# A branch hint, constants as last terms of sums, and a router with fewer vector operations in a fused attention and mixture-of-experts kernel

## The chip, the cores and the metric

One core of one Trainium2 chip. The core has TensorE (PE; its weight loads are shown apart, as PEld), VectorE (DVE), ScalarE (ACT), GpSimd (POOL) and SyncE (SP), which issues most DMAs. Each runs its own list of instructions in order, and semaphores order the lists against each other. The metric is the time of one launch in microseconds (us).

## The reference

Three stages with 4 x 8 heads, 576 tokens a head, 64 wide, so 2304 tokens of 512. Attention has a causal mask and a bias from a running sum of `s`; a softmax row is divided by its sum plus 1e-9. The router takes the largest of 8 logits (`x @ w_gate` plus a bias by the token's modality), and that expert's probability scales the token. Last comes a gated layer.

```python
scores = np.where(causal, -1e9, scores + np.minimum(bias, 0.0))
attn = np.exp(scores - scores.max(-1)); attn /= attn.sum(-1) + 1e-9
logits = x @ w_gate + modality_bias[modality_id]
e_idx = np.argmax(logits, axis=1); probs = softmax(logits)      # its sum + 1e-9
out[e_idx == e] = gate_w * (np.maximum(x @ w1[e], 0) @ w2[e])
out = (sigmoid(x @ w_gate2) * (x @ w_val)) @ w_out
```

## The kernel before, in words

Every product of fp32 numbers is made of three products of a rounded high part and a low remainder, so each operand is split on ACT (high) and on DVE or POOL (low).

**Attention** goes by pairs of heads, 16 of them. The order of its steps is written out by hand: START for the first pairs, then the list PERIOD, gone through once for each pair, with entries shifted by up to four rounds, so that several pairs are under way. `R1` (line 415) adds 1e-9 to the softmax sums of a pair (`rs`), `R2` takes the reciprocal, `N` and `Ns` scale the pair's part of x and of the gate logits (`lg`). `txs` is a matrix product on PE that a router's rank product may ride on. POOL makes the bias tiles (`L174`, `L167`) and the splits of k and v (`L198`, `L202`).

**The router** (`Router.batch`, line 608) runs once for each of 4 batches, after the batch's last `Ns`. It doesn't issue its operations at once: it puts them into a queue, and a `tick` after most DVE steps of PERIOD takes one entry off it. After each operation `gap` empty entries are put in front (1 in batches 0 and 1, 0 in 2 and 3); `space(n)` puts in n more. The operations are: sum of `lg` over head pairs, the modality's bias `tb` added, maximum, one-hot row `oh` of the chosen expert, then `ranks`: with triangular and all-ones matrices PE counts the tokens ahead of each one of its expert. In batches 0 to 2 this product waits for the next `txs` (`side`, `beside`) and holds the queue until then; in batch 3 it is issued where `ranks` stands. Behind it come the copy of the counts, the row number `ix` of each token, the sum of the probabilities and its reciprocal, five indirect table writes on POOL (`tab`, line 675), and two stores of x. In batch 1 a guess of the fullest expert follows (lines 689 to 707), from which the first expert's weights are loaded ahead (`on_guess`). `moe.first` (in period 17) gathers the first rows and splits the first weights on POOL.

**The experts** (`Moe`) take slots of 256 tokens. `early` runs the first two slots, both with the guessed expert; after each of its steps u it calls `main(u)`, which takes all empty entries out of the queue and pumps PUMPS = (9, 0, 0, 14) entries: 9 at u = 0, none at 1 and 2, 14 from 3 on. When the queue is empty, `slots` puts 59 operations in (all at line 774 in the profile), which compute the remaining slots; they must be through by u = 10. `Moe.run` counts its later steps to `last` = 72 and calls `step(u)` behind each; `put(k, ...)` lays a task at step last + k. The last steps, 0 to 8, hold two half slots. `extras` (line 1082) is a block that runs only if there are more tokens for an expert than the main slots hold; otherwise every engine branches over it. Here it isn't run.

**The gated layer** (`Moe2`) follows: Strassen products of 384 tokens (line 1374), the sigmoid on ACT, and the output product (lines 1529, 1580). `preload` loads ACT's table for the sigmoid by an activation of a single column.

Of the kernel before, what the change touches and what calls it, by code (L numbers as in the profile page):

```python
# [54 lines left out]
class Attention:  # L55
# [22 lines left out]
    def setup(self):  # L78
# [23 lines left out]
        for i in range(3):  # L102
            t = self.cp.tile([128, 2, 5], F32, name=f"sums{i}")
            nc.gpsimd.memset(t, 1.0)
            self.sums_t.append(t)
# [193 lines left out]
    def exp(self, n, i):  # L299
        nc, h = self.nc, self.head(n)  # L300
        rows = TS[i]
        nc.scalar.activation(  # L302
            h["P"][i][:rows, : T0[i] + rows], h["P"][i][:rows, : T0[i] + rows], AF.Exp, bias=h["nm", i][:rows], scale=-1.0,
            accum_out=self.sums_t[(n // 2) % 3][:rows, n % 2, POS[i] : POS[i] + 1],
        )
# [107 lines left out]
    def R1(self, p):  # L413
        self.nr[p] = [self.wk.tile([128, 2, 5], F32, tag=t, name=t) for t in ("rs", "ri")]
        self.nc.vector.tensor_scalar(self.nr[p][0], self.sums_t[p % 3], 1e-9, None, ALU.add)

# [79 lines left out]
BF16 = mybir.dt.bfloat16  # L496
SPE = mybir.EngineType.SP
BIG = 100000.0
TROWS, PUMPS = 96, (9, 0, 0, 14)
# [5 lines left out]
class Router:  # L505
    def __init__(self, tc, cp, ap, ps, ident, mod_bias, mod_id, x, tab, B, S):
# [6 lines left out]
        self.oh = [T([128, 6, 8], f"oh{i}", BF16) for i in range(2)]  # L513
        self.lg = [ap.tile([128, 5, 8, 8], F32, name=f"lg{i}") for i in range(2)]
        self.xr = [ap.tile([128, 5, RW], F32, name=f"xr{i}") for i in range(2)]
# [27 lines left out]
        nc.gpsimd.dma_start(self.tab, self.fill[:TROWS])  # L543
        self.cnt = [T([128, 8], f"cnt{i}") for i in range(2)]
        nc.gpsimd.memset(self.cnt[0], 0.0)
        self.k9 = T([128, 9], "k9")
        nc.gpsimd.iota(self.k9, pattern=[[256, 9]], base=128, channel_multiplier=0, allow_small_or_imprecise_dtypes=True)
        self.pidh, self.w256 = T([128, 1], "pidh"), T([128, 1], "w256")
        nc.gpsimd.tensor_copy(self.pidh, self.pid)
        nc.gpsimd.tensor_scalar(self.pidh[HROW : 2 * HROW], self.pid[HROW : 2 * HROW], -float(HROW), None, ALU.add)  # L550
        nc.gpsimd.memset(self.w256, 256.0)
# [53 lines left out]
    def new_x(self, b):  # L605
        return self.xr[b % 2], self.lg[b % 2]

    def batch(self, b, xr, lg):

        nc, cp, T = self.nc, self.cp, self.T  # L610
        V = nc.vector
        oh = self.oh[b % 2]
        cnt, cnt2 = self.cnt[b % 2], self.cnt[(b + 1) % 2]
        tile_ = lambda shape, nm, dt=F32: cp.tile(shape, dt, tag="r_" + nm, name="r_" + nm)
# [6 lines left out]
        L, mx, eq, em = (tile_([128, 5, 8], "L"), tile_([128, 5], "mx"), tile_([128, 5, 8], "eq"), tile_([128, 5], "em"))  # L621
        ex, se = tile_([128, 5, 8], "ex"), tile_([128, 5], "se")
        R, rk = tile_([128, 6, 8], "R"), tile_([128, 5], "rk")
        ix = tile_([128, 5], f"ix{b % 2}", U32)
        c, c1 = tile_([128, 8], "gc"), tile_([128, 8], "gc1")
        iob = self.iota.unsqueeze(1).to_broadcast([128, 5, 8])
        q = self.q
        q.append(lambda: V.tensor_reduce(L.unsqueeze(3), lg, axis=AX.X, op=ALU.add))
        q.append(lambda: V.tensor_tensor(L, L, tb, ALU.add))
        q.append(lambda: V.tensor_reduce(mx.unsqueeze(2), L, axis=AX.X, op=ALU.max))  # L630
# [5 lines left out]
        def mm(rp):  # L636
            if rp is None:
                V.tensor_tensor(R, st["rp"].rearrange("p (t e) -> p t e", e=8), cnt.unsqueeze(1).to_broadcast([128, 6, 8]), ALU.add)
                self.hold = False
                return  # L640
            nc.tensor.matmul(rp, self.tri, oh.rearrange("p t e -> p (t e)"), start=True, stop=False)
            for t in range(5):
                nc.tensor.matmul(
                    rp[:, 8 * t + 8 :].rearrange("p (t e) -> p t e", e=8), self.ones,
                    oh[:, t].unsqueeze(1).to_broadcast([128, 5 - t, 8]), start=False, stop=t == 4,
                )
            st["rp"] = rp
# [11 lines left out]
        self.space(3)  # L659
        q.append(lambda: nc.scalar.activation(ex, L, AF.Exp))  # L660
        self.space(3)
        q.append(lambda: V.tensor_copy(cnt2, R[:, 5]))
        q.append(lambda: V.tensor_tensor(R[:, 0:5], R[:, 0:5], oh[:, 0:5], ALU.mult))
        q.append(lambda: V.tensor_reduce(rk.unsqueeze(2), R[:, 0:5], axis=AX.X, op=ALU.add))
        q.append(lambda: V.scalar_tensor_tensor(out=rk, in0=em, scalar=float(CAP), in1=rk, op0=ALU.mult, op1=ALU.add))
        q.append(lambda: V.tensor_scalar(ix, rk, 8.0 * CAP, None, ALU.add))
        q.append(lambda: V.tensor_reduce(se.unsqueeze(2), ex, axis=AX.X, op=ALU.add))  # L667
        q.append(lambda: V.tensor_scalar(se, se, 1e-9, None, ALU.add))
        q.append(lambda: V.reciprocal(xr[:, :, 512], se))
# [14 lines left out]
        if b == EARLYB - 1:  # L684
# [4 lines left out]
            q.append(lambda: V.tensor_reduce(m, cnt2, axis=AX.X, op=ALU.max))  # L689
            q.append(lambda: V.tensor_tensor(c, cnt2, m.to_broadcast([128, 8]), ALU.is_equal))  # L690
            q.append(lambda: V.scalar_tensor_tensor(out=c, in0=c, scalar=-8.0, in1=self.iota, op0=ALU.mult, op1=ALU.add))
            q.append(lambda: V.tensor_reduce(gf, c, axis=AX.X, op=ALU.min))
            q.append(lambda: V.tensor_scalar(gf, gf, 8.0, None, ALU.add))
            q.append(lambda: V.scalar_tensor_tensor(
                out=self.grow, in0=gf, scalar=float(CAP // 256), in1=self.pid, op0=ALU.mult, op1=ALU.add))
            q.append(lambda: V.tensor_scalar(c1, cnt2, 256.0 * EARLY, None, ALU.max))
            q.append(lambda: V.tensor_tensor(c1, c1, cnt2, ALU.subtract))
            q.append(lambda: V.tensor_tensor(c, self.iota, gf.to_broadcast([128, 8]), ALU.is_equal))
            q.append(lambda: V.tensor_tensor(c, c, c1, ALU.mult))
            q.append(lambda: V.tensor_tensor(cnt2, cnt2, c, ALU.add))  # L700
# [5 lines left out]
            q.append(lambda: self.indices("idx0", self.tid, 16, 576 * EARLYB - 1))  # L706
            q.append(lambda: V.tensor_copy(self.guess_i, gf[0:1]))

# [46 lines left out]
    def slots(self):  # L755
# [6 lines left out]
        V = nc.vector  # L762
        n = self.cnt[self.B % 2]
        gf, pid = self.guess_f, self.pidh
# [10 lines left out]
        op(V.tensor_tensor, cmp, n.unsqueeze(2).to_broadcast([128, 8, 9]), self.k9.unsqueeze(1).to_broadcast([128, 8, 9]), ALU.is_gt)  # L775
        op(V.tensor_scalar, g1, gf, 1.0, None, ALU.add)
        op(V.tensor_reduce, W[:, 0, 1:9].unsqueeze(2), cmp, axis=AX.X, op=ALU.add)
# [112 lines left out]
class Moe:  # L890
# [189 lines left out]
    def extras(self, more, again):  # L1080

        with self.tc.If(more > 0):  # L1082
            tt = self.r.tt
# [672 lines left out]
def kernel(ctx, tc, q, k, v, s, modality_id, moe_w_gate, modality_bias, w1, w2, wg, wv, wo, out):  # L1756
# [10 lines left out]
    with tc.manual_schedule():  # L1767
# [100 lines left out]
        def later():  # L1868
            x, cuts = glu.x_tasks(1, raws1), (0, 3, 7, 9, 12, 15, 18, 18)
            w = [[], [], s0[0], s0[1] + s0[2], s0[3] + s0[4], s0[5], s0[6]]  # L1870
            for k in range(7):
                put(2 + k, w[k] + x[cuts[k] : cuts[k + 1]])
            put(8, [glu.preload])

        put(-5, [first_tokens])
        put(1, [later])
# [53 lines left out]
```

## Time and profile before

| what | us |
|---|---|
| median of 3 runs (lowest, highest) | 940.32 (939.64, 943.79) |
| profiled execution, its own time | 939.85 |
| its span, first to last instruction | 938.1 |
| PE busy | 900.2 |
| DVE busy | 697.7 |
| ACT busy | 548.3 |
| POOL busy | 392.4 |

Busy is a sum over instructions and says nothing of who waits for whom; ends of matmuls are modelled. Attention takes up to about 262 us, the experts to about 515, the gated layer the rest. In timelines a line is the start, the duration, engine, code line and operation, and in brackets the idle time just before it and what ended that. PEclk, or "granted", is TensorE's clock as a share of 2.4 GHz; 0.50 is the lower level, 1.2 GHz.

### The profile page before, as it was taken

How to read it: one execution, taken by the hardware profiler on the slowest of the kernel's cores; microseconds unless marked ns; L12 is line 12 of the kernel's file. 1: busy time of each engine (PE TensorE's matmuls, PEld its weight loads, DVE VectorE, ACT ScalarE, POOL GpSimd, SP SyncE). 2: the span in 40 equal slices, each digit the busy share in tenths (PEclk: the TensorE clock that was granted, in tenths of full speed). 3: DMA queues.
4: the chain of work that ended last, by engine and by line, in shares of the span. 5: the costliest groups of instructions: out<-in, count | busy, mean ns of one | idle time of the engine just before them, and what ended most of it. 6: DMA issues, size and time to landing. Idle time of an engine off the chain costs nothing. (4 is left out here: it accounts for less than half of the span.)

```text
span 938.1 us, 18673 instructions
## 1 busy us (share of the span) xinstructions
PE 900.2 (96%) x6261; PEld 861.7 (92%) x6261; DVE 697.7 (74%) x1569; ACT 548.3 (58%) x1282; POOL 392.4 (42%) x614
## 2 busy tenths in 40 slices
PE   7999999999999999999998899999999999999996
PEld 7899889888899999999987899999999998889996
DVE  5999999999875688867566666767575747868770
ACT  5999899898733656566544555454535345454440
POOL 7988789798642677776610000010001000111111
PEclk9999999999999999999999999999999999999999
DMA  7667559674435558622655322324242308473501
GB/s 174 157 154 168 138 86 130 165 125 121 164 63 88 165 154 263 204 79 81 205 193 201 98 88 87 116 98 129 64 141 79 116 13 299 143 246 98 168 35 45
DMA packets 163871, 125.34 MB, mean 134 GB/s; under 512 B 86737, under 2 KB 147692, under 8 KB 163254
## 3 DMA queue, kind: packets, MB, share of 16 engines
q1 hardware_dynamic: 158566, 112.44, 43.1%
q0 software_dynamic: 3984, 11.32, 4.2%
q8 instruction: 51, 0.84, 0.4%
q14 instruction: 54, 0.44, 0.2%
q10 hardware_dynamic: 1216, 0.30, 0.1%
HBM read 115.95 MB, written 33.23 MB: 159 GB/s over the span
## 5 line engine op out<-in xcount | busy, mean ns | idle before, releaser
L1374 PE MATMUL X<-a,set 128*128 128x384 f32 x864 | 165.7, 340 | 4.1 <-ACTq L1082 3.0
L1374 PEld LDWEIGHTS X<-a,set 128*128 128x128 f32 x864 | 153.1, 189 | 5.9 <-ACTq L1082 3.2
L869 POOL TENSOR_SCALAR dn<-dr 128x256 int8<-128x256 int8 (+1 forms) x60 | 34.1, 569 | 253.7 <-DVE sg L1404 86.4
L932 POOL TENSOR_TENSOR w<-raw,w 128x512 fp32r<-128x512 f32 x56 | 78.9, 1416 | 47.1 <-ACT w L929 44.5
L174 POOL TENSOR_SCALAR bias<-cumB,cumT 128x576 f32<-128x576 f32 (+4 forms) x155 | 82.8, 536 | 24.6 <-DVE nm L293 20.1
L1511 POOL DMA_INDIRECT out_dram<-oy,row x18 | 20.0, 1109 | 169.3 <-ACT oy L1535 92.0
L996 PE MATMUL ph<-xT,w 128*128 128x256 f32 x672 | 89.9, 283 | 0.0
L996 PEld LDWEIGHTS ph<-xT,w 128*128 128x128 f32 x672 | 83.6, 188 | 0.0
L1374 PE MATMUL Y<-a,set 128*128 128x384 f32 x432 | 82.0, 338 | 0.0
L302 ACT ACTIVATE P<-P,nm 128x576 f32<-128x576 f32 (+3 forms) x128 | 79.5, 627 | 2.1 <-DVE nm L293 2.0
L337 DVE TENSOR_TENSOR PL<-pt,PH 128x512 fp32r<-128x512 f32 (+1 forms) x128 | 77.1, 629 | 2.6 <-ACT PH L330 2.2
L1374 PEld LDWEIGHTS Y<-a,set 128*128 128x128 f32 x432 | 76.5, 188 | 0.1
L1383 ACT COPY u<-X 128x384 f32<-128x384 f32 x72 | 34.5, 480 | 61.5 <-PE X L1374 61.4
L293 DVE CUSTOM_DVE_ANT_0 P<-sb,bias 128x320 f32<-128x320 f32 (+3 forms) x128 | 67.2, 548 | 3.2 <-PE sb L284 2.4
L330 ACT CAST PH<-pt 128x512 fp32r<-128x512 f32 (+1 forms) x128 | 64.6, 551 | 7.6 <-PE pt L321 6.2
L321 PE MATMUL pt<-ident,P 128*128 128x128 f32 x448 | 64.6, 278 | 3.6 <-DVE r_se L667 2.0
L932 DVE TENSOR_TENSOR w<-raw,w 128x512 fp32r<-128x512 f32 x56 | 55.0, 982 | 12.2 <-ACT w L929 11.3
L929 ACT CAST w<-raw 128x512 fp32r<-128x512 f32 x112 | 63.6, 620 | 0.0
L1000 ACT ACTIVATE hH<-ph 128x256 fp32r<-128x256 f32 x72 | 27.7, 385 | 61.2 <-PE ph L996 60.1
L284 PE MATMUL sb<-KT,QH 128*128 128x288 f32 (+3 forms) x192 | 56.3, 317 | 6.8 <-DVE nm L293 4.5
L321 PEld LDWEIGHTS pt<-ident,P 128*128 128x128 f32 x448 | 51.0, 141 | 9.7 <-ACT P L302 3.2
L360 PE MATMUL ot<-PH,vhl 128*128 128x512 f32 (+3 forms) x160 | 55.8, 359 | 1.1 <-DVE QL L258 1.0
(318 smaller groups left out, 2385.0 us busy)
## 6 DMA issues: line engine op xcount, KB each, us to landing
raw<-in_moe_w_dram SPq DMA_DIRECT2D x80, 512.0 KB
h<-sg SPq DMA_DIRECT2D x72, 192.0 KB
cumB<-cum_d SPq DMA_DIRECT2D x32, 288.0 KB
hp<-h SPq DMA_DIRECT2D x24, 384.0 KB
qraw<-in_q_dram SPq DMA_DIRECT2D x58, 128.0 KB
dr<-in_moe_w_out_dram SPq DMA_DIRECT2D x12, 511.6 KB
dr<-in_moe_w_gate_dram SPq DMA_DIRECT2D x24, 255.2 KB
dr<-in_moe_w_val_dram SPq DMA_DIRECT2D x24, 255.2 KB
```

The source lines that it names most:

```text
L174: (nc.vector if n in FILLB else nc.gpsimd).tensor_scalar(res[i][:rows], cumB[:rows, :m], -1.0, self.cumT[:rows, i, n : n + 1], ALU.mult, A ...
L284: nc.tensor.matmul(self.sb[:rows, o : o + c1 - c0], X[:, T0[i] : T0[i] + rows], h["KT"][:, c0:c1], start=j == 0, stop=j == 1)
L293: nc.vector.tensor_tensor_reduce(out=pt[:rows, :m], in0=self.sb[:rows, o : o + m], in1=self.bias_t[n][i][:rows], op0=ALU.add, op1=ALU.min, ...
L302: nc.scalar.activation(h["P"][i][:rows, : T0[i] + rows], h["P"][i][:rows, : T0[i] + rows], AF.Exp, bias=h["nm", i][:rows], scale=-1.0, acc ...
L321: nc.tensor.transpose(pt[:, c : c + 128], h["P"][i][:, T0[j] : T0[j] + 128], self.ident)
L330: self.nc.scalar.copy(t[:, :z], pt[:, :z])
L337: self.nc.vector.tensor_tensor(t[:, :z], pt[:, :z], h["H"][u][:, :z].bitcast(F32), ALU.subtract)
L360: nc.tensor.matmul(out[:, q0 : q0 + z - a], w, X[:, a:z], start=k == 0, stop=k == len(mm) - 1, skip_group_check=True)
L929: nc.scalar.copy(v, src)
L932: (eng or nc.vector).tensor_tensor(v, src, h.bitcast(F32), ALU.subtract)
L996: nc.tensor.matmul(ph, w[:, 128 * dc : 128 * dc + 128], x[:, dc], start=k == 0, stop=k == 11)
L1374: self.nc.tensor.matmul(bank, w[:, c], a[:, h, c], start=first and k == 0, stop=k == 5, skip_group_check=True)
```

## The change

- The softmax sums get a second column that holds 1e-9; `R1` is a reduction over the two in place of an addition.
- `lg` gets a ninth term, into which POOL copies the batch's modality bias; the addition behind the reduction goes. A ninth column of `R` holds 8 CAP, and of `ex` 1e-9, so that two more additions go.
- The counts stay in row 5 of `R`, two tiles of which alternate; the copy goes.
- The guess takes nine operations in place of thirteen, in `scalar_tensor_tensor` form; `gf` is now 8 smaller, and users add it back.
- `tc.If(more > 0)` gets a label, and at step 5 SP, PE, DVE and ACT each get an instruction that says that the branch is likely taken. Where the block is skipped, as here, it is.
- `preload` moves from step 8 to step -40.

```diff
@@ -100,8 +100,9 @@
...
         for i in range(3):
-            t = self.cp.tile([128, 2, 5], F32, name=f"sums{i}")
-            nc.gpsimd.memset(t, 1.0)
+            t = self.cp.tile([128, 2, 5, 2], F32, name=f"sums{i}")
+            nc.gpsimd.memset(t[:, :, :, 0], 1.0)
+            nc.gpsimd.memset(t[:, :, :, 1], 1e-9)
             self.sums_t.append(t)
...
@@ -301,7 +302,7 @@
...
             h["P"][i][:rows, : T0[i] + rows], h["P"][i][:rows, : T0[i] + rows], AF.Exp, bias=h["nm", i][:rows], scale=-1.0,
-            accum_out=self.sums_t[(n // 2) % 3][:rows, n % 2, POS[i] : POS[i] + 1],
+            accum_out=self.sums_t[(n // 2) % 3][:rows, n % 2, POS[i], 0:1],
         )
...
@@ -412,7 +413,7 @@
...
         self.nr[p] = [self.wk.tile([128, 2, 5], F32, tag=t, name=t) for t in ("rs", "ri")]
-        self.nc.vector.tensor_scalar(self.nr[p][0], self.sums_t[p % 3], 1e-9, None, ALU.add)
+        self.nc.vector.tensor_reduce(self.nr[p][0].unsqueeze(3), self.sums_t[p % 3], axis=AX.X, op=ALU.add)
...
@@ -495,6 +496,7 @@
...
 SPE = mybir.EngineType.SP
+AHEAD = [SPE] + [getattr(mybir.EngineType, e) for e in ("PE", "DVE", "Activation")]
 BIG = 100000.0
...
@@ -511,7 +513,7 @@
...
         self.oh = [T([128, 6, 8], f"oh{i}", BF16) for i in range(2)]
-        self.lg = [ap.tile([128, 5, 8, 8], F32, name=f"lg{i}") for i in range(2)]
+        self.lg = [ap.tile([128, 5, 8, 9], F32, name=f"lg{i}") for i in range(2)]
         self.xr = [ap.tile([128, 5, RW], F32, name=f"xr{i}") for i in range(2)]
...
@@ -541,12 +543,21 @@
...
         nc.gpsimd.dma_start(self.tab, self.fill[:TROWS])
-        self.cnt = [T([128, 8], f"cnt{i}") for i in range(2)]
-        nc.gpsimd.memset(self.cnt[0], 0.0)
+        self.zero = ap.tile([128, 8], F32, name="zero")
+        nc.gpsimd.memset(self.zero, 0.0)
+        self.R = [p.tile([128, 6, 9], F32, name=f"R{i}") for i, p in enumerate((ap, cp))]
+        for t in self.R:
+            nc.gpsimd.memset(t[:, :, 8], 8.0 * CAP)
+        self.ex = ap.tile([128, 5, 9], F32, name="ex")
+        nc.gpsimd.memset(self.ex[:, :, 8], 1e-9)
         self.k9 = T([128, 9], "k9")
...
         nc.gpsimd.tensor_copy(self.pidh, self.pid)
+        self.pidg = ap.tile([128, 1], F32, name="pidg")
+        nc.gpsimd.tensor_scalar(self.pidg, self.pid, 8.0 * (CAP // 256), None, ALU.add)
+        self.iotam = ap.tile([128, 8], F32, name="iotam")
+        nc.gpsimd.iota(self.iotam, pattern=[[1, 8]], base=-8, channel_multiplier=0, allow_small_or_imprecise_dtypes=True)
         nc.gpsimd.tensor_scalar(self.pidh[HROW : 2 * HROW], self.pid[HROW : 2 * HROW], -float(HROW), None, ALU.add)
...
@@ -605,12 +616,16 @@
...
+    def counts(self, b):
+        return self.R[b % 2][:, 5, 0:8] if b >= 0 else self.zero
+
     def batch(self, b, xr, lg):
...
         oh = self.oh[b % 2]
-        cnt, cnt2 = self.cnt[b % 2], self.cnt[(b + 1) % 2]
+        R = self.R[b % 2]
+        cnt, cnt2 = self.counts(b - 1), self.counts(b)
         tile_ = lambda shape, nm, dt=F32: cp.tile(shape, dt, tag="r_" + nm, name="r_" + nm)
...
@@ -619,14 +634,14 @@
...
         L, mx, eq, em = (tile_([128, 5, 8], "L"), tile_([128, 5], "mx"), tile_([128, 5, 8], "eq"), tile_([128, 5], "em"))
-        ex, se = tile_([128, 5, 8], "ex"), tile_([128, 5], "se")
-        R, rk = tile_([128, 6, 8], "R"), tile_([128, 5], "rk")
+        ex, se, rk = self.ex, tile_([128, 5], "se"), tile_([128, 5], "rk")
         ix = tile_([128, 5], f"ix{b % 2}", U32)
...
         q = self.q
+        q.append(lambda: nc.gpsimd.tensor_copy(lg[:, :, :, 8], tb))
+        self.space(4)
         q.append(lambda: V.tensor_reduce(L.unsqueeze(3), lg, axis=AX.X, op=ALU.add))
-        q.append(lambda: V.tensor_tensor(L, L, tb, ALU.add))
         q.append(lambda: V.tensor_reduce(mx.unsqueeze(2), L, axis=AX.X, op=ALU.max))
...
@@ -635,7 +650,7 @@
...
             if rp is None:
-                V.tensor_tensor(R, st["rp"].rearrange("p (t e) -> p t e", e=8), cnt.unsqueeze(1).to_broadcast([128, 6, 8]), ALU.add)
+                V.tensor_tensor(R[:, :, 0:8], st["rp"].rearrange("p (t e) -> p t e", e=8), cnt.unsqueeze(1).to_broadcast([128, 6, 8]), ALU.add)
                 self.hold = False
...
@@ -657,15 +672,12 @@
...
         self.space(3)
-        q.append(lambda: nc.scalar.activation(ex, L, AF.Exp))
+        q.append(lambda: nc.scalar.activation(ex[:, :, 0:8], L, AF.Exp))
         self.space(3)
-        q.append(lambda: V.tensor_copy(cnt2, R[:, 5]))
-        q.append(lambda: V.tensor_tensor(R[:, 0:5], R[:, 0:5], oh[:, 0:5], ALU.mult))
+        q.append(lambda: V.tensor_tensor(R[:, 0:5, 0:8], R[:, 0:5, 0:8], oh[:, 0:5], ALU.mult))
         q.append(lambda: V.tensor_reduce(rk.unsqueeze(2), R[:, 0:5], axis=AX.X, op=ALU.add))
-        q.append(lambda: V.scalar_tensor_tensor(out=rk, in0=em, scalar=float(CAP), in1=rk, op0=ALU.mult, op1=ALU.add))
-        q.append(lambda: V.tensor_scalar(ix, rk, 8.0 * CAP, None, ALU.add))
+        q.append(lambda: V.scalar_tensor_tensor(out=ix, in0=em, scalar=float(CAP), in1=rk, op0=ALU.mult, op1=ALU.add))
         q.append(lambda: V.tensor_reduce(se.unsqueeze(2), ex, axis=AX.X, op=ALU.add))
-        q.append(lambda: V.tensor_scalar(se, se, 1e-9, None, ALU.add))
         q.append(lambda: V.reciprocal(xr[:, :, 512], se))
...
@@ -687,16 +699,12 @@
...
             q.append(lambda: V.tensor_reduce(m, cnt2, axis=AX.X, op=ALU.max))
-            q.append(lambda: V.tensor_tensor(c, cnt2, m.to_broadcast([128, 8]), ALU.is_equal))
-            q.append(lambda: V.scalar_tensor_tensor(out=c, in0=c, scalar=-8.0, in1=self.iota, op0=ALU.mult, op1=ALU.add))
+            q.append(lambda: V.scalar_tensor_tensor(out=c, in0=cnt2, scalar=m, in1=self.iotam, op0=ALU.is_equal, op1=ALU.mult))
             q.append(lambda: V.tensor_reduce(gf, c, axis=AX.X, op=ALU.min))
-            q.append(lambda: V.tensor_scalar(gf, gf, 8.0, None, ALU.add))
             q.append(lambda: V.scalar_tensor_tensor(
-                out=self.grow, in0=gf, scalar=float(CAP // 256), in1=self.pid, op0=ALU.mult, op1=ALU.add))
-            q.append(lambda: V.tensor_scalar(c1, cnt2, 256.0 * EARLY, None, ALU.max))
-            q.append(lambda: V.tensor_tensor(c1, c1, cnt2, ALU.subtract))
-            q.append(lambda: V.tensor_tensor(c, self.iota, gf.to_broadcast([128, 8]), ALU.is_equal))
-            q.append(lambda: V.tensor_tensor(c, c, c1, ALU.mult))
+                out=self.grow, in0=gf, scalar=float(CAP // 256), in1=self.pidg, op0=ALU.mult, op1=ALU.add))
+            q.append(lambda: V.scalar_tensor_tensor(out=c1, in0=cnt2, scalar=256.0 * EARLY, in1=cnt2, op0=ALU.max, op1=ALU.subtract))
+            q.append(lambda: V.scalar_tensor_tensor(out=c, in0=self.iotam, scalar=gf, in1=c1, op0=ALU.is_equal, op1=ALU.mult))
             q.append(lambda: V.tensor_tensor(cnt2, cnt2, c, ALU.add))
...
@@ -704,7 +712,7 @@
...
             q.append(lambda: self.indices("idx0", self.tid, 16, 576 * EARLYB - 1))
-            q.append(lambda: V.tensor_copy(self.guess_i, gf[0:1]))
+            q.append(lambda: V.tensor_scalar(self.guess_i, gf[0:1], 8.0, None, ALU.add))
...
@@ -760,7 +768,7 @@
...
         V = nc.vector
-        n = self.cnt[self.B % 2]
+        n = self.counts(self.B - 1)
         gf, pid = self.guess_f, self.pidh
...
@@ -773,7 +781,7 @@
...
         op(V.tensor_tensor, cmp, n.unsqueeze(2).to_broadcast([128, 8, 9]), self.k9.unsqueeze(1).to_broadcast([128, 8, 9]), ALU.is_gt)
-        op(V.tensor_scalar, g1, gf, 1.0, None, ALU.add)
+        op(V.tensor_scalar, g1, gf, 9.0, None, ALU.add)
         op(V.tensor_reduce, W[:, 0, 1:9].unsqueeze(2), cmp, axis=AX.X, op=ALU.add)
...
@@ -1079,7 +1087,7 @@
...
-        with self.tc.If(more > 0):
+        with self.tc.If(more > 0, label="more"):
             tt = self.r.tt
...
@@ -1870,8 +1878,9 @@
...
                 put(2 + k, w[k] + x[cuts[k] : cuts[k + 1]])
-            put(8, [glu.preload])
-
+
+        put(-40, [glu.preload])
+        put(5, [lambda: tc.mark_branch_hint_location("more", "LikelyTaken", engines=AHEAD)])
         put(-5, [first_tokens])
...
```

## Rows read from the trace of the kernel before

**Rows 1.** Windows: us, busy us (instructions) of PE, PEld, DVE, ACT, POOL; clock, DMA

```profile
30.00:243.00 213.00, 203.79 (x1516) 186.54 (x1515) 207.36 (x643) 192.32 (x547) 182.98 (x353) 1.00 0.67 146
```

**Rows 2.** Timeline of DVE: the operation `rs` of three of sixteen pairs

```profile
78.47 0.17 DVE L415 TENSOR_SCALAR rs<-sums 128x10 f32<-128x10 f32 x1
...
91.89 0.98 DVE L415 TENSOR_SCALAR rs<-sums 128x10 f32<-128x10 f32 x1
...
108.04 0.17 DVE L415 TENSOR_SCALAR rs<-sums 128x10 f32<-128x10 f32 x1
```

**Rows 3.** Timelines of POOL and of DVE near 98 us

```profile
98.13 1.58 POOL L202 TENSOR_TENSOR vhl<-vraw,vhl 128x640 fp32r<-128x640 f32 x1
...
98.73 1.03 DVE L629 TENSOR_TENSOR r_L<-r_L,tb 128x40 f32<-128x40 f32 x1
```

**Rows 4.** By code line: count, duration in ns (min/median/max), first and last start

```profile
L629 DVE TENSOR_TENSOR r_L<-r_L,tb x4: 190/264/1032, 98.7 to 270.4; 128x40 f32<-128x40 f32 x4
...
L662 DVE COPY cnt<-r_R x4: 151/168/1186, 116.4 to 272.4; 128x8 f32<-128x8 f32 x4
...
L664 DVE TENSOR_REDUCE r_rk<-r_R x4: 175/188/198, 118.8 to 272.7; 128x5 f32<-128x40 f32 x4
...
L666 DVE TENSOR_SCALAR r_ix<-r_rk x4: 172/688/1211, 121.2 to 273.2; 128x5 uint32<-128x5 f32 x4
...
L668 DVE TENSOR_SCALAR r_se<-r_se x4: 164/166/172, 123.7 to 274.8; 128x5 f32<-128x5 f32 x4
...
L697 DVE TENSOR_TENSOR r_gc<-r_gc,cnt x1: 785/785/785, 208.2 to 208.2; 128x8 f32<-128x8 f32 x1
```

**Rows 5.** Timeline of PE and DVE where attention ends and the experts begin

```profile
260.30 1.04 PE L980 MATMUL mtr<-ident,xg 128*128 128x128 f32 x8
...
262.30 1.58 PE L996 MATMUL ph<-xT,ew 128*128 128x256 f32 x11 [0.34 <-DVE xT L986]
...
262.76 0.48 DVE L628 TENSOR_REDUCE r_L<-lg 128x40 f32<-128x320 f32 x1
...
270.44 0.19 DVE L629 TENSOR_TENSOR r_L<-r_L,tb 128x40 f32<-128x40 f32 x1
...
271.84 0.18 PE L641 MATMUL rp<-oh,tri 128*128 128x48 bf16 x1 [0.77 <-DVE oh L634]
```

**Rows 6.** Timeline of ACT and PE at the branch

```profile
515.00 0.59 ACT L1029 COPY yt<-yh 128x512 f32<-128x512 f32 x1 [3.47 <-PE yh L1114]
515.60 1.28 ACT L1278 ACT_TABLE_LOAD   x1
...
517.92 2.19 PE L1374 MATMUL X<-a,set 128*128 128x384 f32 x6 [2.96 <-ACTq L1082]
```

**Rows 7.** Windows: the stretch just behind the branch, columns as in rows 1

```profile
518.00:521.50 3.50, 3.50 (x12) 3.50 (x12) 0.00 (x0) 1.00 (x2) 0.00 (x0) 0.51 0.01 5
```

**Rows 8.** Groups of instructions by line: count | busy us, mean ns | idle before

```profile
L415 DVE TENSOR_SCALAR rs<-sums 128x10 f32<-128x10 f32 x16 | 6.6, 411 | 0.5
```

**Rows 9.** Timeline of POOL: its first instruction behind the setup

```profile
8.50 0.73 POOL L198 TENSOR_SCALAR vhl<-vraw 128x640 fp32r<-128x640 f32 x1 [1.17 <-DVE cumT L129]
```

**Rows 10.** By code line: the branch over the spare slots (q: an engine's sequencer)

```profile
L1082 SPq EVENT_SEMAPHORE  x9: 17/17/17, 519.6 to 520.2; - x9
...
L1082 ACTq EVENT_SEMAPHORE  x2: 17/17/17, 517.9 to 517.9; - x2
...
L1082 PEldq COMPARE_BRANCH  x1: 3357/3357/3357, 513.0 to 513.0; - x1
```

**Rows 11.** Timeline of SP and ACT behind the branch

```profile
520.48 2.11 SPq L1295 DMA_DIRECT2D xs<-x  x4
...
528.04 0.84 ACT L1309 CAST a<-xs 128x768 fp32r<-128x768 f32 x1
```

**Rows 12.** The page's groups: busy us, mean ns | idle before, and what ended it

```profile
L1000 ACT ACTIVATE hH<-ph 128x256 fp32r<-128x256 f32 x72 | 27.7, 385 | 61.2 <-PE ph L996 60.1
```

## The prediction

> **What bounds the kernel now.** I read the busy time of the engines in long windows first. From 30 to 243 us, where attention runs, VectorE (DVE) is busy 207.4 of 213.0 us, TensorE (PE) 203.8, ScalarE (ACT) 192.3, GpSimd (POOL) 183.0 [rows 1]. PE's share flatters it, since ends of matmuls are modelled; DVE has 5.6 us left, so here DVE sets the pace. The timeline of DVE confirms it by the operation `rs`, once in a period (a pair of heads): from 78.47 to 91.89 no router work runs and the period takes 13.42 us; the next, 91.89 to 108.04, holds the first half of batch 0's router work and takes 16.15 [rows 2]. Router work on DVE lengthens attention.
>
> The timelines of POOL and DVE side by side then show why such tiny work is dear: an add of 128x40 takes 1.03 us, and ends as POOL's 1.58 us subtraction ends [rows 3]. By code line, the adds and copies between SBUF tensors run from 0.15 to 1.21 us, while the reduction of the same size never leaves 0.175 to 0.198 [rows 4].
>
> Third, the end of attention [rows 5], where PE takes over as the bound, and fourth the waits at the branch around the spare slots: PE stands for 2.96 us until 517.92 [rows 6], and then the granted clock is 0.51 for 3.5 us [rows 7]. From there to the end the chain of waits is mostly PE.
>
> **DVE work removed.** For a line that ran four times, minimum + twice the median + maximum is the sum. The modality add: 0.190 + 2 x 0.264 + 1.032 = 1.75 us. The copy of the counts 1.67, the last add to the row index 2.76, the add of 1e-9 0.67 [rows 4]; together 6.85. Of that the last batch (about 0.70, all at the minimum) and three operations of batch 2 (about 0.49) lie behind the DVE-bound stretch; 5.65 remain. The sixteen `rs` take 6.6 us [rows 8]; as a reduction of 20 elements I price each at 0.18, from the reduction of 40, so 2.9: 3.7 less, were all inside the stretch; 3.6. The guess loses four operations: a subtraction that takes 0.79, and three that I put at 0.17 each like the cheapest add: 1.3 [rows 4]. Sum 10.55.
>
> Added: the reduction over nine instead of eight terms, 40 elements more, under 0.1 us each: 0.1 in the stretch. And a shift: counting the queue's entries against PERIOD, three entries of batch 1 behind its rank sum and four of the guess go, two ticks each while the gap is 1: 14 ticks. Batch 2's own POOL copy and spaces, less its add, take 4 back. So batch 2 reaches `ranks` 10 ticks earlier; today it misses a `txs` by 2, and then waits for the next. After, it rides that earlier one. Its mask product, rank sum, index, sum and reciprocal then run inside the DVE-bound stretch: five operations from 0.17 up, and held now and then, 1.2. Net 9.3 us of DVE.
>
> How much of it is attention's? Bounds: nothing, if another engine takes over at once, and 9.3. ACT, the next true load, has 20.7 of 213 us left, so there is room for all; but a hold by POOL that misses one operation meets the next between SBUF tensors, and in part the schedule is latency. I take two thirds: **-6.2** (-3 to -9).
>
> The rule that speaks of these holds is in the Trainium skill, "SBUF — State Buffer", section "SBUF: two separate sides": VectorE and GpSimd take a shared port pair as an exclusive lock, for the whole instruction. It names operations with two SBUF inputs, and the guess's three fused operations have two. By it each can be held as the subtraction is (0.79 less 0.17), three times 0.6 and two thirds of that: 1.2 us less gain. The held add agrees with the rule [rows 3]; no run here shows it for a fused operation of that form.
>
> **POOL's copies and constants.** The eight more setup instructions on small tiles lie before POOL's first splitting, which waits 1.17 us at 8.50 today [rows 9]: nothing, unless they take over 0.15 each; the rest of it, at most 0.5, would then show. Four copies of `tb` stand in POOL's stream ahead of `spv`; in batches 0 to 2 DVE asks for them six ticks (some 3 us) later: nothing. In batch 3 no spaces remain (the pump drops them). By the count the five table writes of batch 2 are in POOL's queue well before, so POOL is free; if not, DVE waits and PE behind it.
>
> **What the earlier batch 2 does at the end of attention.** Today main(0) pumps batch 2's five table writes, two stores, the gap and one reduction of batch 3: nine. After, those seven have gone, and the nine reach `ranks`: its six matmuls now stand in PE's stream before the second first-layer product. PE ends its transposes at 260.30 + 1.04 = 261.34 and today goes on fully at 262.30 [rows 5]. After, it must wait for DVE's reduction at 262.76 (0.55 to the next start) and the five operations behind it; today from the modality add at 270.44 to the rank matmul at 271.84 is 1.40, without that add about 1.18: 262.76 + 0.55 + 1.18 = 264.49. With a matmul and the ranks' 0.15 before it the product is 2.4 us late. Where the ranks stand today PE's wait of 0.77 goes, and 0.15 of matmuls: net +1.5. PE's gap of 3.15 us is longer than the 2.96 after which the clock fell at the branch; 3.5 us at half clock cost 1.75 [rows 7]. I take that fall as likely: **+3.2** (+1.5 to +3.5). The slots' arithmetic starts a step earlier, but no wait of PE behind it names the slots: zero.
>
> **The branch.** PE's compare-and-branch takes 3357 ns; ACT's semaphores come at 517.9, SP's from 519.6, each about 3 us after its branch [rows 10]. PE starts X at 517.92 on ACT's semaphore [rows 6]. If the hint brings the target in ahead, PE waits for ACT's last copy, 515.00 + 0.59 = 515.59, since the table load (1.28) moves out; 517.92 - 515.65 = 2.3. A gap of 0.7 us should leave the clock up: 1.75 more [rows 7]. Against it: the next x loads leave SP from 520.48, and ACT reads them at 528.04 [rows 11]. SP can leave only some 2.5 us earlier, as the store of the last slot must land; ACT wants them 4 earlier, so up to 1 us comes back, I take 0.5. **-3.6** (0 to -4.5). The hints themselves, four instructions, are no row of this trace; between 0 and 0.3.
>
> The Trainium skill, "Runtime: NRT & Kernel Launch", section "Instruction fetch mechanics", says that prefetch is purely sequential over two pages and a taken branch outside them waits for a DMA. The 3 us agree; by its word "purely" a hint would bring nothing, which is rival 1.
>
> The table load itself, 1.28 on ACT [rows 6] and an activation, moves 40 steps ahead into the experts. ACT's Relu there waits 60.1 us for PE in 72 times, 0.8 each [rows 12], which hides most of it: **+0.2** (0 to 1.5).
>
> **Sum.** -6.2 + 3.2 - 3.6 + 0.2 = -6.4 against the profiled run's 939.85 (span 938.1): 933.4. The median of the runs lies 0.47 above it, so the forecast is **933.7**.
>
> **Rivals.** (1) The hint does nothing: PE still starts 2.96 us late, the clock still falls. -6.2 + 3.2 + 0.2 = -2.8: 937.5. For it: no row shows a hint. Against: straight code comes in without such gaps, so there is room for a block ahead of need. 0.18. (2) The gain in attention turns into waits for ACT or POOL: -1.5 instead of -6.2, 938.6. For it: ACT at 90%; against: the period without router work is 2.7 us shorter. 0.14. (3) Slower: the hint displaces PE's next block. PE's instruction queue still moves a block between step 5 and the branch; if the target has taken that block's place, PE stands another 3 us there with the clock's 1.75 behind it, and still fetches at the branch. -6.2 + 3.2 + 0.2 + 4.8 = +2.0 on the median 940.3: 942.3. It decides if the hint comes ahead of that crossing and only two blocks are held. Against: such a hint would be useless wherever code is straight. 0.06. (4) The rank matmuls don't stall PE, because batch 2 doesn't catch the earlier `txs`: 933.7 - 3.2 = 930.5. For it: little, the count has a margin of 8 ticks; but the ticks hang on the order of the code alone, and I may have miscounted. 0.10.
>
> **How the numbers follow.** The forecast has 0.52, own range 930.5 to 936.5. The rivals have 0.48. The range 929.5 to 939.5 holds the first, all of (4), (1) and most of (2), and leaves out (3) and edges. Half a per cent (4.7 us), which a measurement of this kernel just tells from no change, puts the bound at 935.6: of the forecast 0.42 lies below, of (4) 0.09, of (1) and (2) 0.05: faster 0.56; slower, over 945, 0.03; the same 0.41.
>
> **What would show it.** Right: `rs` and the index line at 0.2 throughout, periods with router work near 14.5 us, attention over about 6 us sooner; batch 2's rank matmuls one period earlier; batch 3's in front of the second expert product with a PE wait near 3 us and a clock near 0.5 behind; at the branch a PE gap below 1 us and clock 1.0. Wrong: a DVE that falls to 90% busy with the same periods, or a compare-and-branch that still takes 3 us on PE or ACT.

## The result and the profile after

The changed kernel takes **931.30 us** (median of 6 runs, 930.99 to 933.92) against 940.72 of the kernel before (6 runs): ratio 0.9893, 95% interval 0.9875 to 0.9910. The forecast was 933.7, range 929.5 to 939.5. The profiled execution takes 931.2 us, its span is 929.3 (before 939.85 and 938.1).

I cut both spans at the same instructions: the first and the last `rs`, the start of the sixth first-layer product behind the second transposes (277.83 before, 274.64 after), the end of PE's last product ahead of the branch (514.96, 511.74), and the first product behind the branch, X.

| stretch, us | before | after | difference | forecast |
|---|---|---|---|---|
| start to the first `rs` | 35.01 | 36.45 | +1.4 | 0 |
| first to last `rs` (attention) | 222.91 | 214.15 | -8.8 | -6.2 |
| last `rs` to the sixth product | 19.91 | 24.04 | +4.1 | +3.2 |
| sixth product to the last one ahead of the branch | 237.13 | 237.10 | 0.0 | +0.2 |
| that one's end to X | 2.96 | 0.72 | -2.2 | -2.3 |
| X to the end | 420.20 | 416.89 | -3.3 | -1.3 |
| sum | 938.1 | 929.3 | -8.8 | -6.4 |

Windows of the changed kernel, columns as in [rows 1]: attention, where the experts begin, and the stretch behind X.

```profile
36.45:250.60 214.15, 206.17 (x1567) 192.24 (x1566) 201.98 (x647) 195.63 (x555) 188.29 (x356) 1.00 0.66 149
258.80:262.00 3.20, 3.20 (x17) 3.20 (x17) 1.52 (x4) 0.39 (x1) 0.00 (x0) 0.50 0.02 5
513.00:516.50 3.50, 3.50 (x22) 3.50 (x21) 1.26 (x3) 1.96 (x5) 0.00 (x0) 1.00 0.27 77
```

The kernel before, from its first to its last `rs`:

```profile
35.01:257.92 222.91, 212.16 (x1569) 194.07 (x1568) 213.74 (x659) 196.51 (x555) 186.84 (x352) 0.99 0.63 139
```

DVE (third pair) does 11.8 us less there, and attention is shorter by three quarters of that. But the kernel before also has a stretch of half clock inside attention, and the changed one none there:

```profile
248.40:251.80 3.40, 3.40 (x12) 3.01 (x13) 1.40 (x3) 1.31 (x3) 3.23 (x4) 0.50 0.00 0
```

DVE has work for only 1.40 of these 3.40 us, so DVE wasn't the bound here. An estimate from half of the stretch: up to 1.7 of the 8.8 us are due to the clock and not to DVE's work. Behind X the clock is 1.00 in place of 0.51 [rows 7]; where the experts begin it is 0.50.

By code line, the changed kernel's `rs`, one-hot row, subtraction and index (count, ns min/median/max), against [rows 4, 8]:

```profile
L416 DVE TENSOR_REDUCE rs<-sums x16: 160/173/174, 36.4 to 250.6; 128x10 f32<-128x20 f32 x16
L649 DVE TENSOR_TENSOR oh<-iotax,r_em x4: 185/688/1423, 106.6 to 258.2; 128x40 bf16<-128x40 f32 x4
L672 DVE TENSOR_TENSOR r_L<-r_L,r_mx x4: 185/197/235, 108.3 to 258.4; 128x40 f32<-128x40 f32 x4
L679 DVE SCALAR_TENSOR_TENSOR r_ix<-r_em,r_rk x4: 150/155/165, 119.2 to 268.9; 128x5 uint32<-128x5 f32 x4
```

`rs` is never held (a DVE operation is held when it lasts until a POOL operation beside it ends); the index line isn't either. Of the operations that stay, the one-hot row is still held (1.42).

Timeline of PE, ACT and DVE where the experts begin, against [rows 5]:

```profile
252.99 1.04 PE L988 MATMUL mtr<-ident,xg 128*128 128x128 f32 x8
...
254.94 1.07 ACT L993 CAST xT<-mtr 128x512 fp32r<-128x512 f32 x2 [2.60 <-PE mtr L988]
255.56 1.29 DVE L994 TENSOR_TENSOR xT<-mtr,xT 128x512 fp32r<-128x512 f32 x2 [1.50 <-ACT xT L993]
...
256.77 0.52 DVE L644 TENSOR_REDUCE r_L<-lg 128x40 f32<-128x360 f32 x1
...
258.50 0.20 PE L656 MATMUL rp<-oh,tri 128*128 128x48 bf16 x1 [4.48 <-DVE oh L649]
...
258.67 2.86 PE L1004 MATMUL ph<-xT,ew 128*128 128x256 f32 x12
```

The rank product now stands ahead of the second first-layer product. PE waits 4.48 us for `oh`, and the product then takes 2.86 us at half clock (1.60 at full).

Timeline of ACT, PE and SP at the branch, against [rows 6, 11]:

```profile
511.78 0.59 ACT L1037 COPY yt<-yh 128x512 f32<-128x512 f32 x1 [3.47 <-PE yh L1122]
...
512.46 1.32 PE L1382 MATMUL X<-a,set 128*128 128x384 f32 x6 [0.72 <-ACTq L1090]
...
516.15 2.10 SPq L1303 DMA_DIRECT2D xs<-x  x4
...
521.04 0.84 ACT L1317 CAST a<-xs 128x768 fp32r<-128x768 f32 x1
```

By code line, the branch, against [rows 10]:

```profile
L1090 SPq EVENT_SEMAPHORE  x9: 17/17/17, 513.9 to 515.9; - x9
...
L1090 PEldq COMPARE_BRANCH  x1: 397/397/397, 509.8 to 509.8; - x1
```

### The profile page after: what moved, and what is told of

Same layout as the page of the kernel before. It is cut to its first block, busy times and chain, and to the rows that moved or that the text cites. A ratio compares the mean times of both kernels' runs of the same rounds, so it can differ in the third digit from the quotient of the medians.

```text
span 929.3 us, 18666 instructions
## 1 busy us (share of the span) xinstructions
PE 890.6 (96%) x6261; PEld 856.7 (92%) x6261; DVE 687.5 (74%) x1549; ACT 547.2 (59%) x1282; POOL 395.8 (43%) x626
## 5 line engine op out<-in xcount | busy, mean ns | idle before, releaser
L175 POOL TENSOR_SCALAR bias<-cumB,cumT 128x576 f32<-128x576 f32 (+4 forms) x155 | 82.9, 537 | 19.3 <-DVE nm L294 18.3
L1317 ACT CAST hf<-hp 128x768 fp32r<-128x768 f32 x42 | 34.1, 835 | 38.9 <-DVE hp L1319 35.2
```

The source lines that it names most:

```text
L175: (nc.vector if n in FILLB else nc.gpsimd).tensor_scalar(res[i][:rows], cumB[:rows, :m], -1.0, self.cumT[:rows, i, n : n + 1], ALU.mult, A ...
```

## Experiments

Twelve runs in four groups, each group timed in 5 rounds beside the kernel before on one chip; figures are ratios to that kernel with their 95% intervals. Three chips were used (the first two groups share one), and the kernel before had medians of 945.0, 943.7, 939.1 and 942.8 us in the groups. Some stretches vary between executions of like code: the first `rs` comes at 33.8 to 37.5 us in the 14 profiles, and ten of them have a stretch or two of half clock in attention. Attention takes 222.91 and 226.69 us in the two profiles with its old code, 213.80 to 217.89 in the nine with all of its edits.

### The branch alone

```diff
-        with self.tc.If(more > 0):
+        with self.tc.If(more > 0, label="more"):
...
-            put(8, [glu.preload])
+        put(-40, [glu.preload])
+        put(5, [lambda: tc.mark_branch_hint_location("more", "LikelyTaken", engines=AHEAD)])
```

Expected: 

> The kernel before with the branch part alone: label and hints, and preload 40 steps earlier; attention and router as before. Theory: PE's gap at the branch falls from 2.96 to about 0.7 us (-2.2) and the granted clock stays at 1.0 behind it (-1.5 by the changed kernel's trace): -3.8 us, about 936.9, and the part behind 535 us no shorter than before. Rival A: the hint acts only together with the rest: +0.2, 940.9. Rival B: the faster matmuls behind 535 us in the changed kernel (1.2 to 1.8 us) come from the branch part too: -5.5, 935.2.

Measured 0.9955 (0.9937 to 0.9972), -4.3 us. PE's gap is 0.72 us and its compare-and-branch 0.397. The theory's -3.8 fits, so rival 1 of the prediction is out. Attention, the same code as before, took 226.69 us in this profile against 222.91.

### Hint on ACT alone

```diff
-AHEAD = [SPE] + [getattr(mybir.EngineType, e) for e in ("PE", "DVE", "Activation")]
+AHEAD = [mybir.EngineType.Activation]
```

Expected: 

> The changed kernel with the hint on ACT alone. Theory: each engine fetches for itself. PE's own branch takes 3.4 to 3.8 us again, so PE starts X 1.8 to 2.0 us behind its last product instead of 0.72 (+1.2), and SP issues the x loads some 3 us later (at 519 in place of 516) while ACT wants them 8.6 us behind X, so ACT and PE wait up to 4 us for them: +1.2 to +5 against the changed kernel. Rival: only the engine whose release PE waits for matters (ACT): no difference.

Measured 0.9915 (0.9899 to 0.9931) against 0.9886 (0.9862 to 0.9909) of the changed kernel beside it; the intervals overlap, so the loss is plainer in the trace than in the time. Its timeline of ACT and PE, and then PE's branch:

```profile
510.75 0.59 ACT L1037 COPY yt<-yh 128x512 f32<-128x512 f32 x1 [3.47 <-PE yh L1122]
...
512.73 1.29 PE L1382 MATMUL X<-a,set 128*128 128x384 f32 x6 [2.01 <-PEq L1090]
```

```profile
L1090 PEldq COMPARE_BRANCH  x1: 3532/3532/3532, 508.7 to 508.7; - x1
```

PE now waits for its own branch, 2.01 us as expected, though ACT had its hint: each engine needs its own. The wait for the x loads didn't come: SP sent them at 516.31, 3.6 us behind X (3.7 in the changed kernel), and ACT read them at 521.28.

### The changed kernel without the branch part

```diff
-        put(-40, [glu.preload])
-        put(5, [lambda: tc.mark_branch_hint_location("more", "LikelyTaken", engines=AHEAD)])
+        put(8, [glu.preload])
```

Expected: 

> The changed kernel without the hints and with preload back at step 8: attention and router edits alone. Theory: attention ends 7.3 us sooner, of which 4.1 are given back where the experts begin (batch 3's rank matmuls in front of the second first-layer product, a PE wait over 3 us and 3.4 us at clock 0.5): -3.2, 937.5; the gap at the branch is 2.9 us again. Rival: the 1.4 us by which the first rs came later in the changed kernel's trace is chance, then -4.6, 936.1. Rival B: the shorter tail behind 535 us is due to the router: -5.0, 935.7.

Measured 0.9923 (0.9899 to 0.9948), -7.3 us, more than the -3.2 of the theory. Attention took 215.62 us; against the 226.69 of the run with the branch alone, timed together with it, that is -11.1, and PE's wait for `oh` was 3.34. So the theory's number, from one pair of profiles, was too small; attention varies by 4 us between profiles of like code. The gap at the branch was 2.97 us, and this time no half clock followed.

### Ranks out of main(0)

```diff
-TROWS, PUMPS = 96, (9, 0, 0, 14)
+TROWS, PUMPS = 96, (8, 0, 0, 14)
```

On the changed kernel: `main(0)` takes eight entries instead of nine. Expected: 

> The changed kernel with PUMPS (8, 0, 0, 14): main(0) stops ahead of batch 3's ranks, which main(3) issues with the 13 entries behind it. Theory: the rank matmuls' stand cost the 4.1 us: PE's wait of 4.48 us ahead of the second first-layer product falls to about 0.6, the clock stays at 1.0 there (1.75), and no wait comes at step 3, since oh is long ready: 4.3 us less than the changed kernel, 927.0, with the 1.3 us by which the transposes' release came late kept; 925.7 without. Rival: PE waits for something else there (the second half of xT, the gathered rows) or at step 3 instead: less than 1 us of gain, 930.5.

Measured 0.9874 (0.9851 to 0.9896). I then ran the changed kernel twice, the second time with this one beside it. Expected of the three, in that order:

> The changed kernel again, on the chip of the runs beside it. Theory: the parts add up, 0.9955 x 0.9923 = 0.988 of the kernel before, about -11 us; PE's gap at the branch 0.72 us, 20 us from the second transposes to the sixth first-layer product. Rival: the recorded 0.9893 stands, -10, and the parts hide each other in part.

> The changed kernel, beside the next two on one chip. 0.987 to 0.989 of the kernel before; 20 us from the second transposes to the sixth first-layer product.

> PUMPS (8, 0, 0, 14) again, now beside the changed kernel. Theory: the stretch from the second transposes to the sixth first-layer product falls from 20.0 to 20.6 us to between 15.6 and 17.2, so this kernel is 0.4 to 0.5% faster than the changed one, about 0.983 to 0.985 of the kernel before. Rival: what is saved there is lost again by step 10, where the queue of the slots must be through: the same time as the changed kernel.

Measured: changed 0.9886 (0.9862 to 0.9909), as the parts give (0.9955 x 0.9923 = 0.988), and 0.9916 (0.9891 to 0.9941); PUMPS 8 beside the latter 0.9864 (0.9841 to 0.9888), faster by 0.5% in the ratios and by 3.4 us in the medians (931.31, 927.89). Timeline of PE in the second run of PUMPS 8:

```profile
253.69 1.04 PE L988 MATMUL mtr<-ident,xg 128*128 128x128 f32 x8
...
254.96 0.38 PE L1004 MATMUL ph<-xT,ew 128*128 128x256 f32 x1 [0.24 <-ACT xT L993]
255.69 1.58 PE L1004 MATMUL ph<-xT,ew 128*128 128x256 f32 x11 [0.34 <-DVE xT L994]
...
264.31 0.20 PE L656 MATMUL rp<-oh,tri 128*128 128x48 bf16 x1
```

Neither the wait nor the half clock is left, and the rank product in step 3 waits for nothing. From the end of the transposes to the sixth product it takes 15.6 us (17.2 in the first run), against 20.6, 20.0 and 19.3 in the changed kernel and 16.5 before; the three other profiles with PUMPS 8 have 15.6 to 16.0. The theory holds: the rank product's stand cost 3 to 4 us. In this one profile the next stretch, up to the branch, took 241.3 us (236.3 to 239.0 in the others, with half clock at 490.8 us here alone), so it doesn't show the gain as a whole; the medians do.

### The softmax sums alone, and the router with the old ones

```diff
-        self.nc.vector.tensor_scalar(self.nr[p][0], self.sums_t[p % 3], 1e-9, None, ALU.add)
+        self.nc.vector.tensor_reduce(self.nr[p][0].unsqueeze(3), self.sums_t[p % 3], axis=AX.X, op=ALU.add)
```

This edit, with the second column that it needs, on the kernel before; then its reverse on the changed kernel without the branch part, and on PUMPS 8. Expected of the three, in that order:

> The kernel before with the softmax sums' edit alone (rs as a reduction over a second column of 1e-9). rs falls from 6.6 us in sixteen to 2.7. Theory: DVE paces attention, two thirds to all of 3.9 us come back: -2.6 to -3.9, 936.8 to 938.1. Rival: a hold by GpSimd that misses rs meets the next operation on two SBUF tensors: the sum of held time moves elsewhere, -1 or less, 940.

> The changed kernel with the old branch, the old preload and the old rs: the router's edits alone. Theory: rs paces nothing, since a period without router work took 13.4 us whether rs took 0.17 or 1.0: then this kernel comes out as with rs, 0.992 (-7.3 us). Rival: rs is worth the 3.3 us that it was measured at alone, then 0.996 (-4).

> The same with the old rs (an addition on GpSimd-held SBUF operands instead of the reduction). Theory: rs is worth 2 to 4 us (3.3 measured on the kernel before, 4 us of attention between two traces): 0.2 to 0.4% slower than the kernel beside it. Rival: nothing, as the two kernels without the branch part (0.9923 with the new rs, 0.9925 with the old one) say.

Measured: `rs` alone 0.9965 (0.9950 to 0.9981), -3.3 us; its one profile, with half clock at two places of attention (77.8 and 251.8 us), doesn't show it (226.40 us of attention against 226.69 in the run with the branch alone). The router alone 0.9925 (0.9911 to 0.9938), as with the new `rs` (0.9923), on the same chip but not timed together. PUMPS 8 with the old `rs` 0.9907 (0.9884 to 0.9929) against 0.9864 beside it. `rs` in these two, the old one first:

```profile
L415 DVE TENSOR_SCALAR rs<-sums x16: 159/642/1273, 36.5 to 253.5; 128x10 f32<-128x10 f32 x16
```

```profile
L416 DVE TENSOR_REDUCE rs<-sums x16: 160/174/176, 37.5 to 251.3; 128x10 f32<-128x20 f32 x16
```

Neither of the two had a stretch of half clock in attention, which took 216.95 and 213.80 us; the two other profiles without one, with the new `rs`, took 214.15 and 215.01. The two comparisons that were timed together say 3 to 4 us. The third, between two groups, says 0, with room for some 2.6 us either way by its intervals. I take 3, an estimate.

### Where the table load stands

```diff
-        put(-40, [glu.preload])
+        put(8, [glu.preload])
```

On PUMPS 8 with the hints. Expected: 

> PUMPS (8, 0, 0, 14) with the hints, but preload back at step 8. Theory: the table load (1.28) and its activation (0.20) stand in ACT's stream between its last copy and its release of PE, so the gap is 0.72 + 1.48 = 2.2 us: +1.5 against PUMPS 8 with the early preload, +3 where the granted clock falls behind the gap. Rival: with the target there in time the release goes out ahead of the table load: no difference.

Measured 0.9858 (0.9839 to 0.9877) against 0.9874 and 0.9864 at -40, no slower in time, though the trace shows the theory's gap (timeline of ACT and PE, then the window behind X):

```profile
511.24 1.28 ACT L1286 ACT_TABLE_LOAD   x1
...
512.84 1.62 PE L1382 MATMUL X<-a,set 128*128 128x384 f32 x6 [2.23 <-ACTq L1090]
```

```profile
513.70:517.10 3.40, 3.40 (x12) 3.40 (x11) 0.61 (x2) 1.01 (x3) 0.00 (x0) 0.50 0.23 23
```

These were not timed together, and intervals of 2 us each leave room for the 1.5 us of the theory, if hardly for 3; but the load at -40 may cost something too. Timelines of ACT and PE of the changed kernel:

```profile
359.11 1.28 ACT L1286 ACT_TABLE_LOAD   x1
...
370.00 0.39 PE L1024 MATMUL sb<-hL,w 128*128 128x256 f32 x1 [1.52 <-DVE hL L1009]
```

All eight profiles with the load at -40 have this wait (1.42 to 1.64 us), the others 0 to 0.41 there. Some of it may only move: at the next such place, 8 us on, those eight wait 0.72 to 0.83, but the kernel before 1.49 and the run above 1.44. PE of the kernel before:

```profile
379.47 0.39 PE L1016 MATMUL sb<-hL,w 128*128 128x256 f32 x1 [1.49 <-DVE hL L1001]
```

The last run moved the load, on PUMPS 8:

```diff
-        put(-40, [glu.preload])
+        put(-30, [glu.preload])
```

Expected: 

> PUMPS (8, 0, 0, 14) with the hints and preload at step -30 in place of -40. In every trace with preload at -40 PE waits 1.4 to 1.6 us for hL some 11 us behind the table load (near 370 us); with preload elsewhere 0 to 0.4 there. Theory: that wait is the price of the place, since GpSimd's and DVE's int8 decode follows there; at -30, where PE waited nowhere from 385 to 437 us, the load costs under 0.4: PE's wait near 368 us falls to 0.4 or less, the gap at the branch stays 0.72, and the time is 1.1 us shorter than with PUMPS 8, 0.985 of the kernel before. Rival: ACT has no such room anywhere among the experts: the wait of 1.5 us moves along and comes some 11 us behind the load again.

PE's waits for `hL` from 355 to 400 us (sum, count, longest) in this run:

```profile
PE sb L1024 <- DVE hL L1009: 0.8, 1, 0.8
```

The changed kernel in the same stretch:

```profile
PE sb L1024 <- DVE hL L1009: 2.6, 3, 1.5
```

The 1.5 us near 366 are gone, and nothing comes behind the load at 385.69; the 0.8 left stands at 373, ahead of it. In time (0.9862, 0.9832 to 0.9892) a difference of 1 us from PUMPS 8 with the load at -40 can't be told. PUMPS 8 with the load at -40 is the version shown to beat the changed kernel, timed together.

## Why the prediction was right

**Attention, -6.2 forecast, -8.8 measured.** DVE was the bound, as said (the `rs` edit alone, 3.8 us less of DVE, brought 3.3 us), and the share was near (three quarters for two thirds), but the work removed was under-sized: 11.8 us of DVE, not 9.3. The guess went from 5.2 to 2.4 us (2.9 less, 1.3 forecast; three operations that I put at 0.17 took 0.14, 0.41 and 0.52 in the trace before), and the subtraction `r_L<-r_L,r_mx`, which stays and which I left as it was, from 2.71 to 0.81; the one-hot row took back 1.6. Which operation a POOL operation catches changes with every shift, so the sum of holds can't be had from the removed lines alone. `rs` came as priced (2.75 us; 2.9 forecast). And up to 1.7 of the 2.6 us beyond the forecast may be the chance of the clock shown above, which the prediction didn't have.

The sign that I gave for periods with router work, 14.5 us, came only on average. The periods with the first half of batch 0 and 1 took 15.68 and 16.06 us (16.15 and 16.22 before), since the one-hot row was held there (1.18 and 1.42 us); those with the second half both took 13.80 (15.55 and 16.61). Batch 2's ranks ride one `txs` earlier (228.09 us, behind the fourteenth `rs` instead of the fifteenth), as counted: rival 4 is out, and so is rival 2.

By the lock that the Trainium skill tells of ("SBUF — State Buffer", section "SBUF: two separate sides") the guess's fused operations can be held. The traces agree. The three take 0.23, 0.39 and 0.39 us here, and the second ends 0.02 us behind a POOL operation that was under way when it began (timelines of POOL and DVE):

```profile
197.38 1.41 POOL L203 TENSOR_TENSOR khl<-kraw,khl 128x576 fp32r<-128x576 f32 x1
...
198.43 0.39 DVE L706 SCALAR_TENSOR_TENSOR r_gc<-R 128x8 f32<-128x8 f32 x1
```

In two other profiles of this code, where it began earlier in POOL's operation, it took 1.13 and 1.14. The trace before had a held fused operation too (`r_rk<-r_em,r_rk`, 0.72 and 0.71 us in batches 0 and 1, 0.17 in 2 and 3), so the prediction was wrong that no run shows one. The index line, fused as well, is no proof against it: in batches 0 and 1 it began, in all eleven profiles with the new router, when POOL's operation had some 0.13 us left.

**Where the experts begin, +3.2 forecast, +4.1 measured.** The mechanism is the one named; PUMPS 8 takes it away. The wait was 4.48 us for my 3.15; six profiles with the ranks there have 3.15 to 4.48, and half clock behind it each time. The excess in this trace comes ahead of DVE's reduction: ACT starts on the transposes 1.95 us behind their start, before the change 0.64. Over the six profiles the wait is this delay and 2.5 to 2.7 us more: with 0.64 it is 3.15 to 3.34, as forecast. Why PE's release comes late in some is open.

**The branch, -3.6 forecast, -2.2 and -1.5 measured.** The gap fell by 2.24 (2.3 forecast), and the clock stayed up. The 0.5 us for late x loads did not come: ACT read them 8.6 us behind X and 4.9 behind SP's issue, and had no wait for them. But the clock's 1.5 belongs to this pair of profiles: of the four with a gap near 3 us, three show half clock behind it and one doesn't.

The Trainium skill ("Runtime: NRT & Kernel Launch", section "Instruction fetch mechanics") calls prefetch purely sequential. Unhinted branches agree (3.36 us before, 3.53 with the hint on ACT alone); with a hint PE's took 0.397, so that word doesn't hold there.

**The table load, +0.2 forecast, about 0.8 to 1.5 by the waits.** I read the cover from a mean (0.8 us of wait per Relu); the wait, for DVE's `hL`, came 11 us behind the load. The run at -30 and the eight profiles show the load as its cause; the way between isn't traced. This step failed, inside its range. Its size is loose: with the wait 8 us on counted in, the load cost 0.8 us in the recorded pair and some 1.2 on average of the eight profiles against the six. In the recorded pair the whole stretch up to the branch didn't get longer for it (0.0).

**Not foreseen:** +1.4 at the start and -1.8 behind X. The start varies as said, and no run ties it to the change: 35.0 to 36.3 us in the three profiles with the old router, 33.8 to 37.5 in the eleven others. The -1.8 may in part be the change's: from the last of three small waits behind X to the end it took 390.0 us before and 388.3 after, 389.7 to 390.0 in the three profiles with the old router and 387.8 to 389.6 in the eleven with the new one. How the router could act there no run shows.

So the sum came out 2.4 us too high: -2.6 in attention, +0.9 where the experts begin, and +1.4 and -2.0 in the first and the last stretch. That misses of both signs cancel in part is luck. The sum of the prediction has a slip as well: 939.85 less 6.4 and with the 0.47 is 933.9, not 933.7.

## What to carry to other kernels

Price a removed wait by what stands next in the queue's order: a shift by ten ticks here put a product in front of PE's main work and gave back 3 to 4 us that one number (9 to 8) returns. Where an engine holds another's small operations (POOL those of DVE here), count the whole group's time before and after, not the lines removed. A mean wait doesn't show that a place is free; look at the stretch itself.

## What the runs showed of the hardware that was not expected

The hints run at the start, though the code calls for them at step 5. By code line of the changed kernel:

```profile
L1934 ACTq BRANCH_PREFETCH_HINT  x1: 54/54/54, 0.8 to 0.8; - x1
L1934 SPq BRANCH_PREFETCH_HINT  x1: 56/56/56, 0.8 to 0.8; - x1
L1934 DVEq BRANCH_PREFETCH_HINT  x1: 51/51/51, 0.8 to 0.8; - x1
L1934 PEldq BRANCH_PREFETCH_HINT  x1: 50/50/50, 0.9 to 0.9; - x1
```

They take 0.05 us each and still act some 510 us later; the displacement of rival 3 shows nowhere. Without a hint the engines pay in different places: PE in the branch itself (3.3 to 3.8 us), ACT and SP in the semaphores behind it, which come about 3 us after a branch of 0.05 (SP in the trace before: 516.5 and 519.6).
